# Scales of the gate and value weights from a partition's sum of magnitudes on ScalarE, in place of raw maxima on VectorE, with new issue times for that stage

## The chip, the core and the metric

The program runs on one core of a Trainium2 chip. The engines of the core work side by side, each through its own instructions in a fixed order: TensorE (PE, with its weight loads shown as PEld), VectorE (DVE), ScalarE (ACT), GpSimd (POOL) and SyncE (SP), which issues the DMAs here. Time is the device time of one execution in microseconds; less is better. A profiled execution also leaves a trace; its span is the time from the first to the last instruction.

## The reference

Attention whose scores are masked by hash buckets, then a gated feed-forward block, then a second feed-forward block. In the lines that matter:

```python
scores = np.where(mask, scale * np.matmul(q, k.transpose(0, 1, 3, 2)), -1e9)
attn = np.exp(scores - scores.max(-1, keepdims=True)); attn /= attn.sum(-1, keepdims=True) + 1e-9
x = np.matmul(attn, v)                        # 2 batches x 8 heads, 768 x 64 -> 1536 x 512
gate = 1 / (1 + np.exp(-(x @ w_gate)))        # 512 x 1536
x = (gate * (x @ w_val)) @ w_out              # the gate/value stage, then the w_out stage
h = x @ w_in                                  # second block, 512 x 2048
g = np.where(h >= 1, h, np.where(h <= -1, 0, (h + 1) ** 2 / 4))
out = g @ w_out2
```

Inputs are drawn normally; the gate weights are 188.518 times as large as the shapes would suggest.

## The kernel before

**Precision.** A product in full precision is made from 16-bit halves: each operand is split into a high and a low float16 part, and three matmuls (high by high, high by low, low by high, lines 421 to 423) are summed in PSUM. So that the weights keep within float16's range, each tile of weights is multiplied by a power of two. That power comes from the tile's own magnitudes, worked out on the chip.

**The gate/value stage.** The stage has twelve weight tiles, in the order g0, v0, g1, v1, ... g5, v5 (g a gate tile, v a value tile). Each tile is used for both batches, which gives 24 groups of work, numbered k = 0 to 23: k = 0 and 1 are g0, k = 2 and 3 are v0, k = 4 and 5 are g1, and so on. A group is an object `Quad`. It makes four blocks of output by a scheme with seven products instead of eight, `P(0)` to `P(6)`, each six matmuls of 128x384. The products accumulate in PSUM banks called qa, qe, qb, qc and qd. Since one product serves several blocks, ScalarE copies a bank into the next (`seed`: qa to qb, qb to qc, qb to qd, line 386) and keeps qe in SBUF (`keep5`, line 372). TensorE's P(2) waits for the first copy, P(4) for the second and P(6) for the third. VectorE adds (line 402), ScalarE applies the tanh of the gate (line 389), VectorE multiplies (line 392).

**What a weight tile goes through.** The input arrives as two raw tiles `wr` (`a_load`, three DMAs on SP, lines 309 to 312), in 64-bit words whose high and low words are converted into one float32 tile `wt` of 128x1024 on the chip: magnitudes on ScalarE (`a_abs`, line 164, two), range on GpSimd (`w_range`, line 167), a shift on VectorE (line 170), low words (line 173, two) and sign (line 176, two). The scale takes its own way: `a_max` takes the largest raw high word of each partition from each raw tile (two reductions, line 265), joins the two (line 267), and `row_out` sends the 128 numbers by DMA into one row (line 256). `row_in` then reduces that row on VectorE (line 239), masks the exponent (line 240), does three small GpSimd steps (lines 242, 243, 246) and sends the scale by DMA to all partitions (line 261). With `wt` and the scale, `a_sum` makes sums of quarter tiles (`ws`, line 334), `a_hi` writes the high parts on ScalarE (line 342: `a` of 128x768 and two `s` of 128x512), `a_lo` the low parts on VectorE (line 350). The raw tiles have two buffers per kind: gate tiles share one pair, value tiles from v1 on another, so a load waits until the last reader of the tile before it is done.

**What sets the order.** Every step is put on a list with a program time, in units of one product; the list is sorted and the instructions are issued in that order. `on` and `at` put a step on the list. The tables hold the times: `F0`, `AT` and `AM` for the attention's pairs of heads, `QP` for the steps of a group (seeds, sums, acts), `WP` for the steps of a weight tile. A time decides nothing but the place in the engines' queues; on each queue the order is strict, and semaphores hold a waiting instruction and all behind it. The end of attention is written by hand as well: there the first gate groups (k = 0 and 1) are threaded between the last attention steps, the evacuations of the attention output (line 718, VectorE: `xr` from `O`) free the one PSUM bank `O` for the next output, and the casts of line 153 and the subtractions of line 131 split the attention output into high and low parts. For g0 the tile is made long before, within attention. Steps `g_load` and `g_max` (lines 206 and 209) read weights of later stages for their own scales, spread over this stage.

## Time and profile before

| | |
|---|---|
| median of 3 runs | 761.7 us (761.12 to 762.7) |
| profiled execution: time / span | 759.33 us / 757.5 us |
| granted TensorE clock, mean | 0.994 |
| PE busy | 728.7 us, 96% of the span, 4883 matmuls |
| DVE busy | 648.1 us, 86% |
| ACT busy | 521.1 us, 69% |
| POOL busy | 227.5 us, 30% |

TensorE is idle for 28.8 us of the span in all (757.5 less 728.7). The time outside the span is 1.83 us. Attention lasts to about 237 us with the first two gate groups within its end, the gate/value stage to about 404 us, the w_out stage to about 460 us, and the second block to the end.

### The profile page before, as it was taken

What the parts mean: (1) busy time and instruction counts of PE and PEld (TensorE: products, weight loads), DVE (VectorE), ACT (ScalarE), POOL (GpSimd) and SP (SyncE); (2) the same over time, 40 slices, a digit from 0 to 9 for tenths busy, and PEclk for the clock granted to TensorE, in tenths of its full rate; (3) what the DMA queues carried; (4) which work ended last, traced back from release to release, by engine and by line L of the source; (5) the groups of instructions that cost most, each with busy time, mean ns of one, the idle gap of its engine ahead of it and who ended that gap; (6) DMA issues with size and microseconds to landing.
All of it is one profiled execution on the core that took longest, in us unless ns stands there. A gap on an engine that the chain in (4) does not pass through costs nothing.

```text
span 757.5 us, 13220 instructions
## 1 busy us (share of the span) xinstructions
PE 728.7 (96%) x4883; PEld 461.5 (61%) x4883; DVE 648.1 (86%) x1141; ACT 521.1 (69%) x985; POOL 227.5 (30%) x311
## 2 busy tenths in 40 slices
PE   7899999999998999998999999998999999999997
PEld 4778878888885555555555556664555555555553
DVE  6899999889888989998889999999999996766643
ACT  6789889988885674673764445546776677767753
POOL 6435267774685653463430001103000000000000
PEclk9999999999999999999999999999999999999999
DMA  8564554454302155556565913533333200100002
GB/s 253 157 184 113 137 146 121 106 128 100 100 1 56 57 180 197 178 170 209 180 230 199 406 56 112 168 112 113 110 112 94 73 1 29 57 0 1 1 1 83
DMA packets 53200, 89.59 MB, mean 118 GB/s; under 512 B 9872, under 2 KB 33040, under 8 KB 53136
## 3 DMA queue, kind: packets, MB, share of 16 engines
q1 hardware_dynamic: 52400, 88.07, 37.8%
q8 instruction: 38, 0.62, 0.3%
q10 hardware_dynamic: 736, 0.69, 0.3%
q14 instruction: 26, 0.21, 0.1%
HBM read 68.65 MB, written 3.15 MB: 95 GB/s over the span
## 4 chain that ended last, share of the span: by engine, by line
PE 35%; DVE 22%; DMA 4%; ACT 3%; issue 2%; POOL 1%; SPq 1%; ACTq 0%; DVEq 0%; POOLq 0%
DVE h L131 2%; PE p L423 2%; PE p L422 2%; PE p L421 2%; DMA gi<-in_moe_w_in_dram 2%; PE qa L1357 2%; DVE gmx L209 2%; PE qa L1356 2%; PE qa L1355 2%; PE qe L1356 2%; PE qe L1355 2%; PE qe L1357 2%; PE o L1356 2%; PE o L1357 2%; PE o L1355 2%; DVE h L392 2%
## 5 line engine op out<-in xcount | busy, mean ns | idle before, releaser
L643 DVE SCALAR_TENSOR_TENSOR PT<-pt,PT 128x512 f16<-128x512 f32 x144 | 95.2, 681 | 8.5 <-ACT PT L640 7.0
L605 DVE TENSOR_REDUCE st<-sc 128x1 f32<-128x768 f32 x96 | 90.7, 948 | 6.5 <-PE sc L597 5.5
L609 ACT ACTIVATE P<-sc,st 128x768 f32<-128x768 f32 x96 | 87.1, 908 | 8.7 <-DVE st L605 7.9
L640 ACT ACTIVATE PT<-pt 128x512 f16<-128x512 f32 x144 | 82.2, 599 | 11.4 <-PE pt L631 9.7
L631 PE MATMUL pt<-ident,P 128*128 128x128 f32 x576 | 80.9, 279 | 0.8 <-DVE PT L643 0.5
L631 PEld LDWEIGHTS pt<-ident,P 128*128 128x128 f32 x576 | 65.4, 142 | 13.7 <-issue 8.8
L709 PE MATMUL O<-PT,vh 128*64 128x256 f16 x576 | 54.4, 277 | 2.1 <-DVE xr L718 2.1
L421 PE MATMUL p<-y,i 128*128 128x384 f16 x128 | 41.7, 326 | 0.0
L422 PE MATMUL p<-y,i 128*128 128x384 f16 x128 | 41.7, 326 | 0.0
L423 PE MATMUL p<-y,i 128*128 128x384 f16 x128 | 41.7, 326 | 0.0
L709 PEld LDWEIGHTS <-vh 128*64 128x64 f16 x576 | 31.0, 109 | 15.1 <-issue 14.6
L1357 PEld LDWEIGHTS <-g 128*128 128x128 f16 x192 | 18.9, 98 | 25.1 <-DVE g L131 2.3
L709 PE MATMUL O<-PT,vl 128*64 128x256 f16 x288 | 33.8, 273 | 0.0
L242 POOL TENSOR_SCALAR row<-row 1x1 uint32<-1x1 uint32 x15 | 5.5, 369 | 91.0 <-DVE row L240 90.9
L597 PE MATMUL sc<-N,N 128*128 128x384 f32 x96 | 29.3, 386 | 3.1 <-ACT N L533 1.9
L1334 ACT ACTIVATE t<-p,usc 128x384 f32<-128x384 f32 x32 | 21.3, 665 | 15.9 <-PE p L423 15.8
L1355 PEld LDWEIGHTS <-g 128*128 128x128 f16 x192 | 18.9, 98 | 21.3 <-ACT g L1344 1.3
L421 PE MATMUL y<-h,w_o 128*128 128x384 f16 x96 | 31.3, 326 | 0.4 <-DVE h L392 0.4
L1356 PEld LDWEIGHTS <-g 128*128 128x128 f16 x192 | 18.9, 98 | 20.5 <-issue 0.8
L423 PE MATMUL y<-h,w_o 128*128 128x384 f16 x96 | 31.3, 326 | 0.0
L422 PE MATMUL y<-h,w_o 128*128 128x384 f16 x96 | 31.3, 326 | 0.0
L597 PE MATMUL sc<-H,H 128*128 128x384 f32 x96 | 28.9, 382 | 2.3 <-ACT P L609 2.2
(355 smaller groups left out, 2292.8 us busy)
## 6 DMA issues: line engine op xcount, KB each, us to landing
wr_o<-in_moe_w_out_dram SPq DMA_DIRECT2D x28, 512.0 KB, 4.6
gi<-in_moe_w_in_dram SPq DMA_DIRECT2D x21, 384.0 KB, 4.8
gz<-in_moe_w_out_dram SPq DMA_DIRECT2D x21, 384.0 KB, 7.5
go<-in_moe_w_out_dram SPq DMA_DIRECT2D x16, 384.0 KB, 4.6
H<-U SPq DMA_DIRECT2D x28, 192.0 KB, 3.3
wr_i<-in_moe_w_in_dram SPq DMA_DIRECT2D x8, 512.0 KB, 3.8
wr_i<-in_moe_w_in_dram SPq DMA_DIRECT2D x16, 256.0 KB, 3.0
n<-in_qt_dram SPq DMA_DIRECT2D x8, 384.0 KB, 4.3
```

Source lines behind the costliest of these rows:

```text
L421: nc.tensor.matmul(ps, lhsT=wh, rhs=rh, start=first, stop=False, **kw)
L422: nc.tensor.matmul(ps, lhsT=wh, rhs=rl, start=False, stop=False, **kw)
L423: nc.tensor.matmul(ps, lhsT=wl, rhs=rh, start=False, stop=last, **kw)
L605: nc.vector.tensor_reduce(out=self.st[:, 0, self.c:self.c + 1], in_=self.sc[:, :, 0:HN], op=ALU.max, axis=AX.XY, negate=True)
L609: nc.scalar.activation(out=self.P, in_=self.sc[:, :, 0:HN], func=AF.Exp, bias=self.st[:, 0, self.c:self.c + 1], scale=1.0, accum_out=self. ...
L631: nc.tensor.transpose(self.ps[m][:, j, :], un[2 * self.n + e].P[:, a, c:c + 128], ident)
L640: nc.scalar.activation(out=self.part(0, m), in_=self.ps[m], func=AF.Copy, scale=PSCALE)
L643: nc.vector.scalar_tensor_tensor(out=self.part(1, m), in0=self.ps[m], scalar=PSCALE, in1=self.part(0, m), op0=ALU.mult, op1=ALU.subtract)
L709: nc.tensor.matmul(O_ps[r, 0:GN], lhsT=vv[m][:, e, i * D:(i + 1) * D], rhs=PT[:, l, e * NI + i, :], start=(s == 0), stop=(s == len(steps) ...
L1355: nc.tensor.matmul(OA[b][i], lhsT=gh[:, ts], rhs=wh, start=(fc == ORD2[0]), stop=False)
L1356: nc.tensor.matmul(OA[b][i], lhsT=gh[:, ts], rhs=wl, start=False, stop=False)
L1357: nc.tensor.matmul(OA[b][i], lhsT=gl[:, ts], rhs=wh, start=False, stop=(fc == ORD2[-1]))
```

## The change

For the ten tiles g1 to v5 the two reductions and the joining step on VectorE go. In their place ScalarE runs one pass over the finished float32 tile `wt`, with the absolute value as its function and an accumulator that sums each partition's magnitudes (`a_norm`). Its element output goes into the tile's first raw buffer, which nothing reads any more. The row of 128 sums is then treated as a row of float32 numbers: `row_in` is called without the 64-bit form, so `exponents` has two GpSimd steps in place of three, and with 0 in place of 14 as the headroom (`lead`). The tiles g0 and v0 keep `a_max`. The times of the stage are new: loads of gate tiles stand 3.6 and of value tiles 6.2 units earlier, conversions earlier, the row and the scale later, seeds, sums and acts moved; so are the steps around the end of attention, and some in `F0`, `AT`, `AM`. The spacing of the `g_load` and `g_max` steps of the weights "i" goes from 3.1293 to 2.7251.

```diff
+    def a_norm(t):
+        x, raw = wsc[:, a_num(t)], WO[t]["raw"][0]
+        nc.scalar.activation(out=raw.bitcast(F32), in_=WO[t]["wt"], func=AF.Abs, accum_out=x[:, 0:1])
+        row_out(t, x[:, 0:1])
+
     def a_row(t):
-        row_in(t, wsc[:, a_num(t), 2:4], 14.0, True)
+        first = a_num(t) < 2
+        row_in(t, wsc[:, a_num(t), 2:4], 14.0 if first else 0.0, first)
...
             for i in range(2):
-                at(11.9 + 0.65 * i, 0, last, a_abs, "v0", i)
+                at(11.6588 + 0.65 * i, 0, last, a_abs, "v0", i)
                 at(10.8628 + 0.7012 * i, 0, last, a_max, "v0", i)
-            for i, t in enumerate((13.0012, 13.3012, 13.6012, 13.4, 13.85, 14.0)):
+            for i, t in enumerate((12.9754, 13.2754, 14.0754, 13.8742, 16.8242, 17.0000)):
                 at(t, 0, last, a_conv, "v0", i)
...
     for m in range(4):
-        on(7.9432, a_sum, V, "v0", m, True)
-    on(5.7405, a_row, "v0")
-    on(9.4664, a_scale, "v0")
+        on(6.3628, a_sum, V, "v0", m, True)
+    on(4.1807, a_row, "v0")
+    on(5.5893, a_scale, "v0")
...
     QP = {
-        "g": {"seed": (0.4974, 2.358, 4.976), "p5": 3.5377, "sum": (3.99, 5.128, 7.1683, 8.1683), "act": (5.4565, 7.5607, 8.0579, 7.094)},
-        "v": {"seed": (0.3623, 2.8959, 5.4602), "p5": 2.4313, "sum": (3.0782, 5.7535, 7.5389, 6.9122), "act": (3.7144, 5.3665, 5.5617, 6.5916)},
+        "g": {"seed": (0.2651, 2.2467, 4.976), "p5": 3.4485, "sum": (3.99, 5.5247, 6.8017, 8.1683), "act": (5.6194, 7.2386, 8.2511, 6.6591)},
+        "v": {"seed": (0.0402, 2.5738, 5.5827), "p5": 3.5552, "sum": (4.5242, 7.1995, 7.9195, 7.2928), "act": (4.095, 5.5833, 4.7321, 4.9298)},
     }
...
-        "g": {"load": -12.353, "abs": (-7.6756, -6.6904), "conv": (-6.1199, -4.6189, -4.5466, -4.3686, -4.145, -0.7947), "max": (-7.5452, -5.621), "row": -4.3568, "scale": 7.9278, "sum": (-0.0892, 0.724, 1.0886, 3.3024), "hi": (4.4351, 4.7082, 6.3431), "lo": (4.8041, 8.8601, 7.6451)},
-        "v": {"load": -14.3264, "abs": (-6.6935, -4.8952), "conv": (-4.4301, -3.9593, -2.346, 0.2172, -1.0263, 2.9987), "max": (-6.0592, -5.6294), "row": -1.4716, "scale": 9.9234, "sum": (3.1886, 3.5668, 5.287, 4.3833), "hi": (10.4857, 10.7314, 12.6551), "lo": (11.9836, 12.2806, 15.7582)},
+        "g": {"load": -15.9707, "abs": (-12.8785, -9.6904), "conv": (-9.1199, -7.7042, -7.6319, -6.7554, -7.0417, -3.7947), "max": -3.6384, "row": -1.4984, "scale": 6.1142, "sum": (-3.3668, -1.9704, -1.9242, 0.4534), "hi": (4.8637, 5.8088, 7.4437), "lo": (5.4761, 10.7242, 9.9904)},
+        "v": {"load": -20.5181, "abs": (-7.9256, -7.3055), "conv": (-6.2317, -5.7609, -4.8939, -2.091, -3.7825, -1.0482), "max": 0.5348, "row": 5.4491, "scale": 9.753, "sum": (0.4177, 0.7959, 2.287, 1.3833), "hi": (8.9311, 10.3557, 12.6551), "lo": (11.9836, 12.2806, 13.8746)},
     }
...
-        for m, d in enumerate(T["max"]):
-            on(base + d, a_max, n, m)
+        on(base + T["max"], a_norm, n)
```

Lines after the new function stand six higher in the changed program: 386 becomes 392, 342 becomes 348, 718 becomes 724.

**VectorE at the end of attention.** The rows begin where the last weight steps of v0 meet the last attention steps; `xr_2` from `O_3_1` is the evacuation for which the attention's next output waits. Before:

```order
L615 RECIPROCAL st_3_0_4_3353<-st_3_0_4_3353 128x4
L170 TENSOR_SCALAR wt_v_3519<-wt_v_3519 128x1024
L239 TENSOR_REDUCE row_78<-row_78 1x1
L173 SCALAR_TENSOR_TENSOR wt_v_3519<-wr_v_3168,wt_v_3519 128x512
L173 SCALAR_TENSOR_TENSOR wt_v_3519<-wr_v_3167,wt_v_3519 128x512
L643 SCALAR_TENSOR_TENSOR PT_3_2_3434<-pt_2_3548,PT_3_2_3434 128x4x128
L176 SCALAR_TENSOR_TENSOR wt_v_3519<-wr_v_3167,wt_v_3519 128x512
L176 SCALAR_TENSOR_TENSOR wt_v_3519<-wr_v_3168,wt_v_3519 128x512
L240 TENSOR_SCALAR row_78<-row_78 1x1
L334 TENSOR_TENSOR ws_v_3731<-wt_v_3519 128x256
L334 TENSOR_TENSOR ws_v_3731<-ws_v_3731,wt_v_3519 128x256
L718 SCALAR_TENSOR_TENSOR xr_2_3163<-O_3_1_3505,rs_3_1_3_3490 128x256
```

And now:

```order
L170 TENSOR_SCALAR wt_v_3505<-wt_v_3505 128x1024
L649 SCALAR_TENSOR_TENSOR PT_3_2_3434<-pt_2_3548,PT_3_2_3434 128x4x128
L173 SCALAR_TENSOR_TENSOR wt_v_3505<-wr_v_3168,wt_v_3505 128x512
L173 SCALAR_TENSOR_TENSOR wt_v_3505<-wr_v_3167,wt_v_3505 128x512
L239 TENSOR_REDUCE row_78<-row_78 1x1
L176 SCALAR_TENSOR_TENSOR wt_v_3505<-wr_v_3167,wt_v_3505 128x512
L240 TENSOR_SCALAR row_78<-row_78 1x1
L724 SCALAR_TENSOR_TENSOR xr_2_3163<-O_3_1_3507,rs_3_1_3_3490 128x256
```

The evacuation now stands in front of the second sign step and of all four sums of v0.

**ScalarE where the second gate group (k = 1) begins.** The last rows before the copy of qa into qb, on which TensorE's P(2) waits. Before:

```order
L153 CAST pT_1_3599<-xT_1_3314 128x384
L389 ACTIVATE h_0_3557<-h_0_3557,wsc 128x384
L386 ACTIVATE qb_3728<-qa 128x384
L389 ACTIVATE h_0_3557<-h_0_3557,wsc 128x384
L389 ACTIVATE h_0_3557<-qd_3675,wsc 128x384
L153 CAST pB_1_3715<-xr_2_3163 128x384
L153 CAST pT_1_3718<-xt_3313 128x384
```

And now:

```order
L153 CAST pT_1_3596<-xT_1_3314 128x384
L395 ACTIVATE h_0_3557<-h_0_3557,wsc 128x384 x2
L395 ACTIVATE h_0_3557<-qd_3675,wsc 128x384
L153 CAST pT_1_3716<-xt_3313 128x384
L164 ACTIVATE wt_g_3724<-wr_g_3619 128x512
L392 ACTIVATE qb_3738<-qa 128x384
```

One tanh has become two in front of the copy, and a third tanh, a cast and a magnitude step have come to stand ahead of it.

**ScalarE in the second group of a gate tile (k = 5, tile g1).** From the first copy of this group to that of the next. Before:

```order
L386 ACTIVATE qb_4050<-qa 128x384
L389 ACTIVATE h_1_3964<-h_1_3964,wsc 128x384 x2
L386 ACTIVATE qc_4073<-qb_4050 128x384
L342 ACTIVATE a_v_4092<-wt_v_3887,wsc 128x768
L372 ACTIVATE p_g_1_4094<-qe 128x384
L342 ACTIVATE s_v_4096<-ws_v_4006,wsc 128x512
L386 ACTIVATE qd_4104<-qb_4050 128x384
L389 ACTIVATE h_1_4040<-qa,wsc 128x384
L342 ACTIVATE s_v_4096<-ws_v_4006,wsc 128x512
L389 ACTIVATE h_1_4040<-qd_4104,wsc 128x384
L386 ACTIVATE qb_4142<-qa 128x384
```

And now:

```order
L392 ACTIVATE qb_4049<-qa 128x384
L395 ACTIVATE h_1_3954<-h_1_3954,wsc 128x384
L348 ACTIVATE a_v_4066<-wt_v_3874,wsc 128x768
L392 ACTIVATE qc_4074<-qb_4049 128x384
L348 ACTIVATE s_v_4084<-ws_v_3967,wsc 128x512
L272 ACTIVATE wr_g_3933,wsc<-wt_g_3981 128x1024
L378 ACTIVATE p_g_1_4088<-qe 128x384
L392 ACTIVATE qd_4098<-qb_4049 128x384
L395 ACTIVATE h_1_4040<-qa,wsc 128x384
L348 ACTIVATE s_v_4084<-ws_v_3967,wsc 128x512
L395 ACTIVATE h_1_4040<-qd_4098,wsc 128x384
L392 ACTIVATE qb_4136<-qa 128x384
```

The new pass for g2 (line 272) and the high parts of v1 now stand between the copies into qc and qd.

**SP between two weight loads.** Rows of the DMA queue up to the load of gate tile g3; `row_76` there is the scale row of v2. Before:

```order
L256 DMA row_76<-wsc 1x128x1
L206 DMA go_4235<-in_moe_w_out_dram 128x384
L206 DMA go_4272<-in_moe_w_out_dram 128x384
L261 DMA wsc<-row_76 128x1x2
L309 DMA wr_g_4313<-in_moe_w_gate_dram 128x4x128
L311 DMA wr_g_4314<-in_moe_w_gate_dram 128x2x128
L312 DMA wr_g_4314<-in_moe_w_gate_dram 128x2x128
```

And now, where `row_78` is the scale row of g2 and `row_76` again that of v2:

```order
L261 DMA wsc<-row_78 128x1x2
L206 DMA go_4148<-in_moe_w_out_dram 128x384
L206 DMA go_4182<-in_moe_w_out_dram 128x384
L206 DMA go_4224<-in_moe_w_out_dram 128x384
L315 DMA wr_g_4260<-in_moe_w_gate_dram 128x4x128
L317 DMA wr_g_4261<-in_moe_w_gate_dram 128x2x128
L318 DMA wr_g_4261<-in_moe_w_gate_dram 128x2x128
L206 DMA go_4266<-in_moe_w_out_dram 128x384
L256 DMA row_76<-wsc 1x128x1
L206 DMA go_4308<-in_moe_w_out_dram 128x384
L206 DMA go_4344<-in_moe_w_out_dram 128x384
L261 DMA wsc<-row_76 128x1x2
```

The load of g3 stood behind the scale of v2 and now stands in front of it.

## Rows read from the trace of the kernel before

**Rows 1.** The page: busy time of each engine, share of the span, instructions.

```profile
PE 728.7 (96%) x4883; PEld 461.5 (61%) x4883; DVE 648.1 (86%) x1141; ACT 521.1 (69%) x985; POOL 227.5 (30%) x311
```

**Rows 2.** Waits of PE, whole span: who waited for whom, us, times, longest.

```profile
PE qb L421 <- ACT qb L386: 3.6, 3, 2.2
...
PE qb L421 <- ACT qc L386: 1.2, 3, 0.8
...
PE qb L423 <- DVE s_g L350: 0.5, 1, 0.5
```

**Rows 3.** Windows: stretch, length, then busy us (count) of PE, PEld, DVE, ACT, POOL.

```profile
270.00:290.00 20.00, 20.00 (x125) 12.02 (x124) 17.88 (x33) 15.69 (x30) 11.31 (x15) 1.00 0.57 186
```

**Rows 4.** Groups of DVE by line, 239 to 404 us: count, busy us, mean ns.

```profile
L265 DVE TENSOR_REDUCE wsc<-wr_g 128x1 f32<-128x512 f32 x10 | 6.7, 680 | 1.8 <-DMA wr_g<-in_moe_w_gate_dram 1.6
```

**Rows 5.** Timeline of ACT, weight tile v0's high parts: start, length.

```profile
247.45 0.93 ACT L342 ACTIVATE a_v<-wt_v,wsc 128x768 f16<-128x768 f32 x1
248.28 0.71 ACT L342 ACTIVATE s_v<-ws_v,wsc 128x512 f16<-128x512 f32 x1
```

**Rows 6.** Timeline of ACT in attention: an accumulator's read, the next instruction.

```profile
63.85 0.21 ACT L609 ACTIVATION_READ_ACCUMULATOR P<-sc,st 128x1 f32 x1
64.07 0.90 ACT L609 ACTIVATE P<-sc,st 128x768 f32<-128x768 f32 x1
```

**Rows 7.** Timeline of ACT at a late load; in brackets the idle time before.

```profile
358.45 0.68 ACT L164 ACTIVATE wt_g<-wr_g 128x512 f32<-128x512 f32 x1 [2.41 <-DMA wr_g<-in_moe_w_gate_dram]
359.02 0.58 ACT L389 ACTIVATE h<-qd,wsc 128x384 f32<-128x384 f32 x1
359.96 0.69 ACT L164 ACTIVATE wt_g<-wr_g 128x512 f32<-128x512 f32 x1 [0.36 <-DMA wr_g<-in_moe_w_gate_dram]
360.53 0.51 ACT L386 ACTIVATE qb<-qa 128x384 f32<-128x384 f32 x1
```

**Rows 8.** Timeline of SP's queue ahead of that load.

```profile
352.46 0.48 SPq L261 DMA_DIRECT2D wsc<-row  x1
...
353.67 0.38 SPq L309 DMA_DIRECT2D wr_g<-in_moe_w_gate_dram  x1
```

**Rows 9.** Timeline of PE at the end of attention and in k = 1.

```profile
237.49 0.30 PE L709 MATMUL O<-PT,vh 128*64 128x256 f16 x2 [2.11 <-DVE xr L718]
...
244.42 0.32 PE L421 MATMUL qb<-pT,s_g 128*128 128x384 f16 x1
...
249.42 0.34 PE L421 MATMUL qd<-pT,a_g 128*128 128x384 f16 x1 [0.66 <-ACT qd L386]
```

**Rows 10.** Timeline of DVE ahead of that evacuation, and two later sums.

```profile
233.41 2.78 DVE L176 SCALAR_TENSOR_TENSOR wt_v<-wr_v,wt_v 128x512 uint32<-128x512 uint32 x2
...
236.22 0.42 DVE L334 TENSOR_TENSOR ws_v<-wt_v 128x256 f32<-128x256 f32 x1
...
237.02 0.42 DVE L718 SCALAR_TENSOR_TENSOR xr<-O,rs 128x256 f32<-128x256 f32 x1
...
243.73 0.55 DVE L402 TENSOR_TENSOR h<-qc,p_g 128x384 f32<-128x384 f32 x1
```

**Rows 11.** Timeline of ACT at the start of k = 1.

```profile
243.90 0.47 ACT L386 ACTIVATE qb<-qa 128x384 f32<-128x384 f32 x1
```

**Rows 12.** DMA issues, 240 to 400 us: count, KB each, median us to landing.

```profile
row<-wsc SPq DMA_DIRECT2D x10, 0.5 KB, 1.9
wsc<-row SPq DMA_DIRECT2D x10, 1.0 KB, 2.3
```

**Rows 13.** Timeline of ACT at the start of the w_out stage.

```profile
402.51 0.72 ACT L1115 ACTIVATE w_o<-wf_o,hsc 128x512 f16<-128x512 f32 x1 [3.08 <-DVE wf_o L176]
```

**Rows 14.** Timeline of PE: attention's second pair, and the second block.

```profile
52.74 0.62 PE L597 MATMUL sc<-N,N 128*128 128x384 f32 x2 [1.03 <-ACT P L609]
...
517.26 0.61 PE L1357 MATMUL qa<-w,g 128*128 128x512 f16 x1 [1.83 <-DVE g L131]
```

**Rows 15.** Window around the second of these; last three: granted clock, DMA share, GB/s.

```profile
516.00:520.00 4.00, 2.74 (x7) 1.04 (x8) 3.97 (x10) 2.94 (x6) 0.09 (x1) 0.59 0.43 131
```

More of the change, by code (lines that the diff above doesn't have):

```diff
@@ L792, in lsh_attention_glu_act @@
             F0 = {
-                "max": (0.835, 4.3363, 4.8113, 6.0),
+                "max": (0.6194, 4.3363, 4.8113, 6.0),
                 "first": (1.1116, 1.92, 2.6321, 2.6521),
@@ L800, in lsh_attention_glu_act @@
                 "MAX": (-0.86, 0.21, 0.88, 1.91, 2.7, 4.3082, 4.6882, 5.3482, 7.3656, 9.7482, 9.8482, 8.9617),
-                "EXP": (0.22, 0.6565, 1.1565, 2.5865, 2.8165, 4.4, 4.86, 7.05, 8.14, 10.5074, 11.21, 9.27),
[1 row of a table removed]
+                "EXP": (0.22, 0.6565, 1.1565, 2.5865, 2.8165, 4.4, 4.86, 6.3485, 8.14, 10.5074, 11.21, 9.27),
[1 row of a table added]
                 "HI": (1.61, 2.61, 4.28, 4.75, 2.76, 6.16, 4.82, 7.1271, 8.1731, 9.03, 9.58, 10.42, 9.66, 11.6, 11.38, 12.5, 12.62, 12.77),
[1 row of a table removed]
[1 row of a table added]
                 "ST": (4.8549, 8.95, 13.1659),
@@ L825, in lsh_attention_glu_act @@
             AM = {
-                "QK": (-1.6212, -0.312, 0.1234, 1.0922, 0.2911, 4.4841, 2.6311, 3.1388, 4.9681, 7.5662, 8.3203, 9.8239),
+                "QK": (-1.6212, -0.312, 0.1234, 1.0809, 0.2911, 4.4841, 2.6311, 3.1388, 4.9681, 7.5662, 8.3203, 9.8239),
                 "MAX": (-0.8384, -0.282, 0.274, 2.0221, 1.7029, 4.7833, 2.832, 3.457, 5.7284, 8.6318, 8.8402, 9.9223),
-                "EXP": (-0.0169, 0.1389, 0.7054, 2.7327, 1.7202, 5.1256, 3.1579, 4.9368, 7.4948, 9.0696, 9.801, 10.9635),
+                "EXP": (-0.0169, 0.1389, 0.7054, 2.7327, 1.7202, 5.1256, 3.1579, 4.6699, 7.4948, 9.0696, 9.801, 10.9635),
                 "T": (0.6726, 2.7818, 2.4903, 2.8259, 5.6069, 4.8189, 4.5978, 6.1506, 6.3992, 8.0591, 8.0212, 8.3198, 10.1114, 11.2138, 10.6646, 10.8685, 12.1144, 12.284),
[1 row of a table removed]
[1 row of a table added]
                 "LO": (2.054, 4.2198, 3.2826, 5.2606, 7.9391, 5.7821, 5.4721, 7.5402, 7.967, 9.0285, 8.7977, 9.5983, 10.7969, 12.174, 11.1739, 12.0774, 12.8392, 13.9848),
@@ L846, in lsh_attention_glu_act @@
                 "V4": (8.2939,),
-                "RB": (7.5895, 9.9185, 12.8309),
-                "VR": (7.1203,),
-                "VT": (10.3243,),
-                "STP": (6.1912, 6.7323, 11.461),
+                "RB": (7.5895, 8.88, 11.7924),
+                "VR": (6.0818,),
+                "VT": (9.2858,),
+                "STP": (5.1527, 6.7323, 11.461),
             }
@@ L1406, in lsh_attention_glu_act @@
         on(6.0 + 0.1 * i, x_op, 1, op, C0, P, True)
-    on(8.106, x_op, 1, "hB22", C1, nc.scalar, True)
-    on(8.3, x_op, 1, "lB22", C1, V, True)
-    on(8.2, x_op, 1, "hT4", C1, nc.scalar, True)
-    on(8.4715, x_op, 1, "lT4", C1, V, True)
+    on(8.4549, x_op, 1, "hB22", C1, nc.scalar, True)
+    on(8.598, x_op, 1, "lB22", C1, V, True)
+    on(5.9953, x_op, 1, "hT4", C1, nc.scalar, True)
+    on(6.0085, x_op, 1, "lT4", C1, V, True)
     for m in range(4):
-        on(7.9432, a_sum, V, "v0", m, True)
@@ L1413, in lsh_attention_glu_act @@
-    on(5.7405, a_row, "v0")
-    on(9.4664, a_scale, "v0")
+        on(6.3628, a_sum, V, "v0", m, True)
+    on(4.1807, a_row, "v0")
+    on(5.5893, a_scale, "v0")
     on(11.1344, a_hi, "v0", "a", 0, True)
-    on(11.4975, a_lo, "v0", "a", 0, True)
+    on(12.195, a_lo, "v0", "a", 0, True)
     for m in range(2):
-        on(11.1514 + 3.1136 * m, a_hi, "v0", "s", m, True)
-        on(11.5944 + 3.0944 * m, a_lo, "v0", "s", m, True)
+        on(10.7952 + 3.0212 * m, a_hi, "v0", "s", m, True)
+        on(11.2174 + 2.7382 * m, a_lo, "v0", "s", m, True)
@@ L1423, in lsh_attention_glu_act @@
     }
     WP = {
-        "g1": {"abs": (-1.9247, -3.3264), "conv": (-1.6834, -1.2227, 2.2696, 1.9568, 2.5568, 2.5305), "max": (-5.2173, -4.5384), "row": 0.0204, "scale": 8.7461, "sum": (3.1461, 4.5686, 3.894, 5.4285), "hi": (11.5982, 11.5142, 12.628), "lo": (12.1178, 11.9436, 16.9718)},
-        "g": {"load": -12.353, "abs": (-7.6756, -6.6904), "conv": (-6.1199, -4.6189, -4.5466, -4.3686, -4.145, -0.7947), "max": (-7.5452, -5.621), "row": -4.3568, "scale": 7.9278, "sum": (-0.0892, 0.724, 1.0886, 3.3024), "hi": (4.4351, 4.7082, 6.3431), "lo": (4.8041, 8.8601, 7.6451)},
@@ L1427, in lsh_attention_glu_act @@
-        "v": {"load": -14.3264, "abs": (-6.6935, -4.8952), "conv": (-4.4301, -3.9593, -2.346, 0.2172, -1.0263, 2.9987), "max": (-6.0592, -5.6294), "row": -1.4716, "scale": 9.9234, "sum": (3.1886, 3.5668, 5.287, 4.3833), "hi": (10.4857, 10.7314, 12.6551), "lo": (11.9836, 12.2806, 15.7582)},
+        "g1": {"abs": (-6.2649, -7.6772), "conv": (-6.0342, -5.5735, -2.0812, -1.2283, -0.3001, -0.4695), "max": 0.9384, "row": 3.5384, "scale": 9.6277, "sum": (0.1461, 1.5513, 0.8767, 3.6183), "hi": (12.1986, 12.1146, 13.2626), "lo": (13.5502, 12.3696, 17.4819)},
@@ L1458, in lsh_attention_glu_act @@
     end = 14 * NT
-    for w, (t0, dt) in {"o": (29.7834, 3.4864), "i": (86.3431, 3.1293), "z": (154.0638, 2.0141)}.items():
+    for w, (t0, dt) in {"o": (29.7834, 3.4864), "i": (86.3431, 2.7251), "z": (154.0638, 2.0141)}.items():
         for k in range(g_num(w)):
```

4 lines of the change are left out of this document (2 added, 2 removed), and 12 rows, old and new, of tables (AM, AT).

## The prediction, made before the changed kernel was run

> **What bounds the kernel now.** I read the page first: TensorE is busy 96% of the span, VectorE 86%, ScalarE 69% [rows 1]. So time can be won only where TensorE stands still (28.8 us in all), and lost wherever a new wait reaches it. Next came the list of what TensorE waits for, and the timeline around each wait. In the gate/value stage the reader is to see that VectorE is almost never the one waited for: the longest such wait is one of 0.5 us, while the copies of the banks on ScalarE (qa to qb, qb to qc) cost 3.6 and 1.2 us [rows 2]. The timeline of ScalarE tells why. At 358.45 and 359.96 the magnitude steps of a gate tile have waited 2.41 and 0.36 us for a load, and the copy into qb stands behind them [rows 7]; TensorE lost 2.19 us there, the longest wait of the first row [rows 2]. SP's queue shows why the load was late: it was issued at 353.67, right behind the scale DMA of the value tile at 352.46 [rows 8]. Of the waits on qb and qc (4.8 us), I found 3.6 us (2.19, and two shorter) behind such late loads. At the end of attention two more waits stand out: 2.11 us for an evacuation on VectorE and 0.66 us for a copy into qd [rows 9].
>
> **What is removed.** Ten tiles lose two reductions of 0.68 us each [rows 4], 13.6 us of VectorE (the small joining steps aside). Worth on the path: hardly more than the 0.5 us wait of row s_g [rows 2], since elsewhere VectorE's idle time hides it. I take 0.7 us, for that wait and two shorter ones on VectorE; bounds 0 and 0.9.
>
> **What is added.** One pass of 128x1024 on ScalarE for each of the ten tiles, with an accumulator. No such pass is in the trace. The 128x768 pass takes 0.93 us and the next instruction starts 0.83 us after it; a 128x512 pass takes 0.71 [rows 5]. So 256 elements more cost 0.22 us, and 1024 take about 0.83 + 0.22 = 1.05 us of the queue. Attention's EXP, which has an accumulator too, is followed by a read that holds the queue from 63.85 to 64.07, 0.22 us [rows 6]. Bounds are 1.05 and 1.27; I take 1.2, nearer to the row with a read. Ten are 12 us of ScalarE, in a stage where a stretch without any wait of TensorE has ScalarE busy 15.7 of 20 us [rows 3].
>
> Does it fit? In that stretch 125 matmuls fill 20 us, 0.16 us each, so a group of 42 lasts 6.7 to 6.8 us. In the second group of a gate tile ScalarE now has three copies, four tanh, one 128x768 pass, two 128x512 passes, one copy of qe and the new pass between one copy into qb and the next. In queue time (each about 0.08 to 0.1 less than its length) that is 3 x 0.41 + 4 x 0.49 + 0.83 + 2 x 0.62 + 0.4 + 1.2 = 6.9 us [rows 5, 7, 11], just over the group. The new pass and the high parts stand between the copies into qc and qd, so the copy into qd ends 0.1 to 0.6 us after P(6) could start. A tanh can slip into the next group, so it does not pile up. Five such groups, at about 0.16: a loss of 0.8 us; bounds 0 and 2.5. A value tile's pass stands in the first group of a gate tile, between the copies into qb and qc, where no high part stands: by the same count 0.1 to 0.8 us are free there. I set it at nothing; without that cover it would be 0.1 to 0.5 us for each of five.
>
> The Trainium skill, "ScalarE: Activation LUTs", section "What ACT_TABLE_LOAD costs", gives an ACTIVATE with immediates as 186 ns and 0.833 ns an element, with about 93 ns of overlap between neighbours. The rows' slope (0.22 us for 256) agrees; by the page alone the pass would be an estimated 0.95 us of the queue, the group 6.6 us, and the loss of 0.8 nothing, so that the time would be 756.7.
>
> **The scale comes later.** The sum needs the finished tile, so row, exponent and scale follow the second sign step. The two DMAs land after 1.9 and 2.3 us [rows 12]; with the reduce and the small steps between them about 5 to 6 us pass from the new pass to the scale. VectorE stands at the reduce of the row (line 239) for up to 2 us; behind it wait sums and products of banks that come due later, and the removed 1.36 us a tile cover most of that. SP stands at line 256 and line 261 as it did before. GpSimd has one small step less a tile. All this I set at nothing; if the scale of a value tile is late, its first high part is, and the sum loses up to 0.5 us a tile.
>
> **Loads.** A gate tile's load no longer stands behind the value tile's scale, but behind the scale of the gate tile before, with three other loads between; that is most of a group earlier. Its buffer is free once the new pass and the sign steps of the tile before are done, which is ahead of that scale. So the late loads vanish, though ScalarE's magnitude steps have moved earlier too. Gain 3.5 us of 3.6; bounds 2.5 and 3.6.
>
> **The end of attention.** The evacuation at 237.02 stood behind two sign steps (2.78 us for both) and two sums of 0.42 [rows 10]. One sign step and both sums now stand behind it: 1.39 + 0.84 = 2.2 us earlier, and the 2.11 us wait goes [rows 9]. But TensorE then runs into the copy into qb for k = 1. Before, that copy began at 243.90 right after one tanh, and P(2) at 244.42 [rows 9, 11]. Now it stands behind a second tanh, which needs the sum that ended at 244.28 (243.73 + 0.55) [rows 10], a third tanh, a cast and a magnitude step. Taking 2.11 off that sum gives 242.17; then 0.5 + 0.5 + 0.4 + 0.6 for these, and 0.47 for the copy, end near 244.65. P(2) starts near 244.7, 0.27 us later than before, so the whole 2.11 is spent in a new wait of some 2.4 us. The wait of 0.66 for qd goes, since P(6)'s copy is no longer behind two weight passes. In k = 2 and k = 3 more is late: the low part of v0 comes behind line 170 of g1, which waits for GpSimd, and TensorE loses 0 to 0.5 us; the new pass of g1 waits for its last sign step, with the copy into qc behind it, 0 to 0.8 us. Taking the middles: 0.66 - 0.27 - 0.25 - 0.45 = -0.3 us. Bounds: -1.5 and +2.1, the latter if the copy is not held.
>
> **The rest.** The conversion of the w_out weights moves up; ScalarE waited 3.08 us for it with the copy into qb behind [rows 13], which cost TensorE 0.84 us. Gain 0.8; bounds 0 and 0.84. In attention's second pair the reductions of g0 stand later in VectorE's queue and no longer delay a row maximum; a wait of 1.03 us [rows 14] shrinks by some 0.4 (bounds 0 and 1). The other moved steps of attention keep their places but for a few neighbours: nothing, within 0.5 either way.
>
> **Sum.** 3.5 + 0.7 - 0.8 - 0.3 + 0.8 + 0.4 = 4.3 us. Against the profiled execution (span 757.5 and 1.83 around it, 759.33 us) that gives 755.0. The median of the runs is 2.4 us above that execution, so I take the same off the median: 761.7 - 4.3, rounded to **757.5**.
>
> **The rivals.** (a) *The queue of ScalarE takes it back: no measurable change.* For: ScalarE's second gate group is full by my count, and the pass waits for a sign step in front of two copies. Against: the 3.6 us of late loads are long single waits, and the new ones would be short. With 0.5 us in each of five groups (2.5) and the end of attention at -1.5, the gain is 3.5 + 0.4 + 0.8 - 4.0 = 0.7: 761.0.
>
> (b) *Slower: the second gate group is bound by ScalarE.* Place: the copies into qc and qd behind the new pass. If the pass waits for its sign step in each gate tile and for the scale in each value tile, 0.8 us for each of ten, it loses 8 against at most 5: 764.5. It decides from about 0.6 us for each of ten. Against: a gate tile's conversion begins 5 units earlier than before, so its sign step should be done.
>
> (c) *The clock.* In the second block a wait of 1.83 us [rows 14] has the granted clock at a mean of 0.59 over 4 us [rows 15], which costs 0.41 x 4 = 1.6 us of matmuls, while the waits of 2.11 and 2.19 us fell at full clock. The new 2.4 us wait at k = 1 could bring the low level, 1.2 GHz in place of 2.4: 757.5 + 1.6 = 759.1. The Trainium skill, "TensorE: Matmul & The Clock Gate", section "HAM oscillation — how this bites in real kernels", says that idle gaps throttle the clock again; the trace agrees at 516 us and not at the other two.
>
> (d) *The end of attention gains its 2.1.* If the copy into qb comes in time: 757.5 - 2.4 = 755.1, and 753.5 if the second gate groups lose nothing besides.
>
> **How the numbers follow.** The forecast with its own spread (756 to 759) has 0.45, (c) 0.10, (d) 0.18, (a) 0.16, (b) 0.11. Faster by over 0.2% (1.5 us, about what a measurement of this kernel can tell from no change) are the forecast, (c) and (d), and a little of (a): 0.75. Within 0.2% is most of (a): 0.14; slower is (b): 0.11. The range goes from 753.5, the end of (d), to 762, just past (a); it leaves out (b) and a few in 100 below.
>
> **What would show it.** Right: no wait of ScalarE for a gate load; no wait of about 2 us for the evacuation, and one of about 2.4 us at P(2) of k = 1; the new pass at 1.1 us with a read of 0.2; waits of TensorE for the copy into qd below 0.6 us in the second gate groups. Wrong: many waits of TensorE on qc or qd behind line 272, high parts of value tiles that wait for the scale DMA, ScalarE still idle for loads, or a clock below full after k = 1.

## The result, and the profile after

The changed kernel takes 753.4 us (752.45 to 754.25, 4 runs), the kernel before 762.2 us (761.12 to 764.0) in the same comparison: ratio 0.9879, 95% interval 0.9857 to 0.9902, so 7.5 to 10.9 us faster. In a second comparison of the same two kernels the ratio was 0.9902 (0.9874 to 0.9930). The forecast was 757.5 in a range from 753.5 to 762, so 753.4 lies just outside it. The direction was right; the gain was about twice the forecast.

The two profiled executions stand 6.73 us apart (759.33 and 752.60). The busy times differ little but for VectorE, ScalarE and GpSimd; the line answers to [rows 1]:

```profile
PE 727.3 (97%) x4883; PEld 461.7 (61%) x4883; DVE 639.5 (85%) x1111; ACT 530.9 (71%) x1005; POOL 220.5 (29%) x301
```

VectorE's busy time falls by 8.6 us only, though reductions of 13.6 us are gone: other steps of the stage took longer, such as the twelve low parts `s_v` (line 356), with a mean of 888 ns in place of 735. Why they did is open.

What TensorE waits for, whole span (columns as in [rows 2]):

```profile
PE qb L427 <- ACT qb L392: 2.3, 1, 2.3
...
PE qd L427 <- ACT qd L392: 1.2, 4, 0.4
...
PE qb L427 <- ACT qc L392: 0.6, 3, 0.3
```

The 3.6 us behind late loads (2.19, 0.85 and 0.58) are gone, and so is the 0.5 us for s_g. The first line is a new wait at k = 1, forecast at 2.4 us. Of the four waits in the second line, three are for the copy into qd in second gate groups: 0.17, 0.32 and 0.32 us, 0.81 in all, where 0.8 was forecast. The fourth, 0.38 us, is in the last value group.

ScalarE at the start of k = 1, then TensorE's P(2) (timeline; answers to [rows 9, 11]):

```profile
240.21 0.61 ACT L395 ACTIVATE h<-h,wsc 128x384 f32<-128x384 f32 x1 [0.32 <-DVE h L408]
240.73 0.56 ACT L395 ACTIVATE h<-qd,wsc 128x384 f32<-128x384 f32 x1
241.19 0.50 ACT L153 CAST pT<-xt 128x384 f16<-128x384 f32 x1
241.59 0.66 ACT L164 ACTIVATE wt_g<-wr_g 128x512 f32<-128x512 f32 x1
242.15 0.48 ACT L392 ACTIVATE qb<-qa 128x384 f32<-128x384 f32 x1
...
242.69 0.32 PE L427 MATMUL qb<-pT,s_g 128*128 128x384 f16 x1 [2.33 <-ACT qb L392]
```

The copy ends at 242.63 behind the tanh, cast and magnitude step that the change put in front of it. The granted clock then falls; the window after it answers to [rows 15]:

```profile
243.00:248.00 5.00, 5.00 (x23) 2.56 (x21) 5.00 (x8) 3.44 (x8) 1.79 (x2) 0.66 0.36 124
```

A mean of 0.66 over 5 us, between the two levels of 1.2 and 2.4 GHz, is up to 1.7 us of matmuls lost. So in this trace the fall of the clock of rival (c) came on top of the wait that the forecast had; its time, 759.1, did not.

The second group of tile g1 (timeline of ScalarE):

```profile
273.78 0.47 ACT L392 ACTIVATE qc<-qb 128x384 f32<-128x384 f32 x1
274.19 0.70 ACT L348 ACTIVATE s_v<-ws_v,wsc 128x512 f16<-128x512 f32 x1
274.80 1.04 ACT L272 ACTIVATE wr_g<-wt_g 128x1024 f32<-128x1024 f32 x1
275.75 0.19 ACT L272 ACTIVATION_READ_ACCUMULATOR wr_g<-wt_g 128x1 f32 x1
275.84 0.47 ACT L378 ACTIVATE p_g<-qe 128x384 f32<-128x384 f32 x1
276.21 0.47 ACT L392 ACTIVATE qd<-qb 128x384 f32<-128x384 f32 x1
```

The new pass holds the queue from 274.80 to 275.84, 1.04 us with its read, which is the lower of the bounds that the prediction gave (1.05), where it took 1.2.

Where the 6.73 us are, by places that both traces have: attention from the small matmul of line 655 (now 661) near 18 us to the third-last evacuation, then the first product of v0 (250.48 and 249.24), then the first product of the w_out stage into its bank `y` (411.31 and 405.70), 2 to 2.5 us after that stage's first products of all:

| part | before | after | gain | forecast |
|---|---|---|---|---|
| start | 18.65 | 18.41 | 0.24 | 0 |
| attention | 206.78 | 205.08 | 1.70 | 0.4 |
| end of attention, k = 0 and 1 | 25.05 | 25.75 | -0.70 | 0.4 |
| k = 2 to the w_out stage | 160.83 | 156.46 | 4.37 | 3.5 |
| the rest | 346.2 | 345.1 | 1.1 | 0 |

(The forecast's terms are put to the rows: 0.66 - 0.27 for the end of attention; 3.5 + 0.7 - 0.8 + 0.8 and the 0.7 lost in k = 2 and 3 for the row below.) The last row is the clock: the 1.83 us wait of [rows 14] is there after the change too, but the clock stays at its upper level behind it this time. Over all the traces of this document, the last part takes 346.2 to 346.6 us in the five with that fall and 344.0 to 345.1 in the twelve without.

Attention's 1.70 us have a second place besides the one forecast. VectorE near 103 us, before and after:

```profile
103.09 0.96 DVE L605 TENSOR_REDUCE st<-sc 128x1 f32<-128x768 f32 x1 [0.40 <-PE sc L597]
103.97 1.75 DVE L176 SCALAR_TENSOR_TENSOR wt_g<-wr_g,wt_g 128x512 uint32<-128x512 uint32 x1
105.64 0.68 DVE L643 SCALAR_TENSOR_TENSOR PT<-pt,PT 128x512 f16<-128x512 f32 x1
```

```profile
100.73 0.68 DVE L649 SCALAR_TENSOR_TENSOR PT<-pt,PT 128x512 f16<-128x512 f32 x1
101.33 1.20 DVE L176 SCALAR_TENSOR_TENSOR wt_g<-wr_g,wt_g 128x512 uint32<-128x512 uint32 x1
102.45 0.94 DVE L611 TENSOR_REDUCE st<-sc 128x1 f32<-128x768 f32 x1
```

A sign step of g0 stood behind a row maximum and held up what followed; now it stands in the gap ahead of that maximum, where VectorE waited 0.40 us, and takes 1.20 in place of 1.75.

### The profile page after: what moved, and what is told of

It is laid out like the page before. It is cut to its first block, busy times and chain, and to the rows that moved or that the text cites. A ratio compares the mean times of both kernels' runs of the same rounds, so it can differ in the third digit from the quotient of the medians.

```text
span 750.8 us, 13224 instructions
## 1 busy us (share of the span) xinstructions
PE 727.3 (97%) x4883; PEld 461.7 (61%) x4883; DVE 639.5 (85%) x1111; ACT 530.9 (71%) x1005; POOL 220.5 (29%) x301
## 4 chain that ended last, share of the span: by engine, by line
PE 33%; DVE 13%; DMA 2%; ACT 1%; issue 1%; SPq 0%; POOL 0%; ACTq 0%
PE p L427 2%; PE p L429 2%; PE p L428 2%; DVE h L131 2%; PE qa L1363 2%; PE o L1363 2%; PE qa L1362 2%; PE o L1362 2%; PE o L1361 2%; PE qa L1361 2%; PE qe L1363 2%; PE qe L1362 2%; PE qe L1361 2%; DMA gz<-in_moe_w_out_dram 1%; DVE w_o L1124 1%; DVE vmx L1215 1%
## 5 line engine op out<-in xcount | busy, mean ns | idle before, releaser
L1121 ACT ACTIVATE w<-wf_z,gsc 128x512 f16<-128x512 f32 x16 | 11.5, 721 | 25.0 <-DVE wf_z L176 25.0
```

## The experiments

Times are medians; a ratio is always to the kernel before, in the same comparison. "The stage" is the time from the first product of v0 to the first one into `y` in the run's own trace, as in the table.

### The kernel before, again

> The kernel before, unchanged, traced a second time. Spread theory: the executions differ by how long the late loads hold ScalarE and by whether the TensorE clock falls, so a second trace shows other sums than 3.6 us behind late loads (up to 6 us), and the median stays 2 to 3 us above the 759.3 us of the first trace. Rival, a fixed offset between a traced and an untraced execution: the same 3.6 us of stalls again, and every trace near 759.

760.76 us (758.6 to 765.82), ratio 1.0001 (0.9974 to 1.0028). Its trace has a span of 762.9 us, 5.4 longer than the first, and other late loads. The waits of TensorE from 245 to 416 us, and one of them with its neighbour on TensorE:

```profile
PE qb L421 <- ACT qb L386: 6.1, 4, 2.7
...
303.98 0.48 PE L421 MATMUL qb<-pT,s_g 128*128 128x384 f16 x1 [2.73 <-ACT qb L386]
304.25 0.53 PE L422 MATMUL qb<-pT,s_g 128*128 128x384 f16 x1
```

```profile
303.00:309.00 6.00, 5.02 (x21) 2.60 (x21) 5.51 (x11) 4.54 (x9) 2.64 (x4) 0.72 0.26 71
364.00:370.00 6.00, 5.22 (x22) 2.72 (x22) 4.53 (x10) 4.48 (x10) 2.11 (x3) 0.72 0.35 108
```

6.1 us where the first trace had 3.6 in that line (0.84 us of each is the start of the w_out stage), and behind two of the waits the clock falls to a mean of 0.72 over 6 us, 1.7 us each. The stage takes 165.62 us against 160.83. So the two traces differ as the spread theory had it, by late loads and by the clock behind them, and the first trace was one of the shorter executions. The median came 1.4 us above it, not 2 to 3.

### The changed kernel, again

> The changed kernel, unchanged, traced a second time. Theory that the change takes out the waits which vary from run to run (late loads in front of the copies of banks): its runs spread over less than 4 us where those of before spread over 9.5 (757.24 to 766.73), the median is 752 to 755, and no wait of ScalarE for a gate load is over 0.5 us in the second trace. Rival, a lucky first set: a spread like that of before and a median of 755 to 758.

753.69 us (752.1 to 754.43), ratio 0.9902 (0.9874 to 0.9930); stage 158.80 us. No wait of ScalarE for a gate or value load appears in its trace. The 6 runs spread over 2.3 us, the 23 of before in the same comparison over 7.5 (757.03 to 764.52).

### Attention's moved steps alone

The new tables F0 and AM and the new list of g0's steps go into the kernel before, nothing else; of the edit only the list is shown:

```diff
-                q, t = ((1, 1.3756), (1, 2.5756), (1, 5.1058), (2, 2.7058), ...
+                q, t = ((1, 2.1099), (1, 3.3099), (1, 5.8401), (2, 2.7058), ...
```

> The kernel before with only the new tables F0 and AM and the new steps of g0 within attention. Theory that these moves pay by themselves: 1.5 to 2.1 us faster than before, all of it by 150 us of the span (about 0.7 at 46 to 56 us, about 1.0 at 103 to 108 us). Rival, that the prediction's 0.4 us was right and the rest came by chance from run to run: 0 to 0.5 us.

759.97 us, ratio 0.998 (0.996 to 1.0001): 1.5 us faster, 0 to 3, with an interval that just takes in no change. In the trace attention takes 204.27 us, against 205.66 in the second trace of before, which has the clock at the same level at 25 us as this one. So 1.4 us, nearer to the new theory than to 0.4.

### The changed kernel with attention's old steps

The reverse edit, in the changed kernel.

> The changed kernel with the old tables F0 and AM and the old steps of g0 in attention. If the new ones pay by themselves: 1.3 to 2.1 us slower than the changed kernel, 755 to 756, all of it before 150 us of the span. Rival, chance from run to run: within 0.5 us of it.

754.5 us, ratio 0.9907 (0.9882 to 0.9932): 0.8 to 1.1 us over the two medians of the changed kernel, with intervals that overlap. Attention takes 205.39 us, 1.46 more than in the second trace of the changed kernel (203.93). The place is settled by the traces; the size by clock time only roughly.

### Load times alone

```diff
-        "g": {"load": -12.353,
+        "g": {"load": -15.9707,
-        "v": {"load": -14.3264,
+        "v": {"load": -20.5181,
```

> The kernel before with only the two load times of the changed kernel, so that a gate load stands in front of the value tile's scale DMA. Stall theory: the waits on qb behind late loads go (3.6 us in the first trace), 2.5 to 5 us faster than before. Rival, the loads are held by the DMA engines and not by their place in the queue: the same waits of ScalarE for a gate load, 0 to 1 us.

760.35 us, ratio 0.9989 (0.9968 to 1.0009): no gain that can be told. ScalarE no longer waits for gate loads, but TensorE has new waits for the low part a_v (3.26, 1.04 and 0.54 us), and behind the longest the clock falls (a mean of 0.69 from 337.5 to 343). SP's queue and VectorE show why:

```profile
328.99 0.38 SPq L309 DMA_DIRECT2D wr_v<-in_moe_w_val_dram  x1
...
330.53 0.50 SPq L256 DMA_DIRECT2D row<-wsc  x1
...
335.37 0.27 DVE L239 TENSOR_REDUCE row<-row 1x1 f32<-1x128 f32 x1 [2.74 <-DMA row<-wsc]
```

The row of 0.5 KB, issued behind a whole weight load, lands 4.8 us later, where the median was 1.9 [rows 12]; VectorE stands for it with the low parts behind. The place of the loads alone only moves the wait.

### The new times with the raw maxima, late and early

Both are the changed kernel with `a_max` in place of `a_norm`, and with the row in its 64-bit form again; first the maxima stand at the place of the pass, then at their old times. The central lines of the second edit:

```diff
-        on(base + T["max"], a_norm, n)
+        for m, d in enumerate(T["max"]):
+            on(base + d, a_max, n, m)
```

> The changed kernel with the raw maxima on VectorE again, at the place of the new pass, so that the new times stand without the new source of the scale. Stall theory (the gain is earlier loads and moved steps, VectorE is hardly waited for): within 1.5 us of the changed kernel, 7 to 10 us faster than before; it may even be faster, since ScalarE loses 12 us of work. Rival, VectorE's relief is what pays: 3 us or more of the gain go, with waits of TensorE on VectorE of over 2 us in the stage.

> The changed kernel with the raw maxima on VectorE at their old times, all other new times kept, so that the scale is ready early and VectorE carries its 13.6 us again while ScalarE is free of the new pass. If VectorE's relief is what makes the new times work: the waits of the run with late maxima stay for the most part (copies into qc and qd held behind sums of VectorE, 4 us or more), 758 to 762. If only the late place of the maxima held up that run: within 1.5 us of the changed kernel, 752 to 755.

762.0 us, ratio 1.0012 (0.9995 to 1.0030), and 761.41 us, ratio 1.0006 (0.9987 to 1.0025). The whole gain is gone in both, though both keep the attention steps; the stage takes 165.88 and 166.24 us, where the old times with the maxima had 160.83 and 165.62. In the first run ScalarE waits for no gate load any more, and still TensorE loses 6.8 us in four waits for copies into qc. My stall theory, by which the new times earn the gain, falls. One wait of the second run, on VectorE and ScalarE:

```profile
302.38 0.69 DVE L173 SCALAR_TENSOR_TENSOR wt_g<-wr_g,wt_g 128x512 uint32<-128x512 uint32 x1
302.99 0.68 DVE L265 TENSOR_REDUCE wsc<-wr_g 128x1 f32<-128x512 f32 x1
303.59 0.55 DVE L407 TENSOR_TENSOR h<-qc,p_g 128x384 f32<-128x384 f32 x1
```

```profile
304.17 0.61 ACT L394 ACTIVATE h<-h,wsc 128x384 f32<-128x384 f32 x1 [1.40 <-DVE h L407]
305.50 0.93 ACT L347 ACTIVATE a_v<-wt_v,wsc 128x768 f16<-128x768 f32 x1 [0.72 <-DMA wsc<-row]
306.34 0.47 ACT L391 ACTIVATE qc<-qb 128x384 f32<-128x384 f32 x1
```

A tanh waits 1.40 us for a sum that stands behind a maximum, the high part waits 0.72 us for its scale (0.15 to 0.53 us in the first trace of the changed kernel), and the copy into qc stands behind both: TensorE loses 1.93 us, and the view puts it down to ScalarE.

### The kernel before without its maxima

```diff
     def a_max(t, h):
+        if a_num(t) > 1:
+            if h == 1:
+                row_out(t, wsc[:, 0, 0:1])
+            return
```

> The kernel before with the maxima of the ten tiles g1 to v5 left out: their rows are sent from the column of g0, so the scales of these tiles are g0's. Old times, old loads. Relief theory (VectorE's 13.6 us hold up sums, conversions and the scale row, and through them ScalarE and the next load): the stage from the first product of v0 to the first of w_out falls from about 162 us (three traces: 160.8, 165.6, 159.7) to 158 or less, 3 us or more faster than before. The prediction's reading (VectorE hardly waited for): late loads stay, 0 to 1 us faster.

755.37 us, ratio 0.9934 (0.9906 to 0.9962): 2.9 to 7.2 us faster; stage 157.84 us. Old times, old loads, no pass on ScalarE, and the gain of the stage is there. A late load is there too, and TensorE waits behind it:

```profile
354.53 0.67 ACT L164 ACTIVATE wt_g<-wr_g 128x512 f32<-128x512 f32 x1 [1.73 <-DMA wr_g<-in_moe_w_gate_dram]
...
357.64 0.32 PE L425 MATMUL qb<-pT,s_g 128*128 128x384 f16 x1 [1.95 <-ACT qb L390]
```

So this gain is not that the late loads vanish. At this place the wait was 2.19 us before. Three other waits stand in both traces alike (0.50, some 0.85 and 0.38 us); what else TensorE waited in the stage comes to 2.2 us in the first trace of before (0.58 for qb, 1.16 for qc, 0.44 for VectorE) and to 0.15 us here. But here SP's queue is free of a wait too, so two more runs part VectorE's queue from that wait.

### Maxima that nobody waits for, and copies in their place

In the first the maxima are computed and the row is sent from g0's column; in the second each tile has one copy of 128 numbers at the place of the last maxima step. Both have g0's scale in ten tiles.

```diff
-            row_out(t, x[:, 0:1])
+            row_out(t, x[:, 0:1] if a_num(t) < 2 else wsc[:, 0, 0:1])
```

```diff
+            if h == 1:
+                nc.vector.tensor_copy(out=x[:, 0:1], in_=wsc[:, 0, 0:1])
+                row_out(t, x[:, 0:1])
+            return
```

> The kernel before, in which VectorE still computes the maxima of the ten tiles, but their rows are sent from the column of g0, so that SP's queue and the scales do not wait for them. If what the removal pays is the wait of SP's queue for the maxima (46.1 us in nine waits in the first trace, with the next loads behind): as fast as the run without maxima, 755 to 757. If it is VectorE's 13.6 us themselves: like before, 760 to 762.

> The kernel before, in which each tile's three maxima steps are one copy of 128 numbers (g0's column) on VectorE at the place of the last of them, so that SP's queue still waits for VectorE, which has 13 us less to do. If VectorE's time is what pays: as fast as the run without maxima, 755 to 757. If it is the wait of SP's queue by its place in the order: nearer to before, 758 to 761.

761.79 us, ratio 0.9997 (0.9975 to 1.0018), and 755.38 us, ratio 0.9922 (0.9891 to 0.9953). So it is VectorE's queue that pays, and not SP's wait. What these runs do not part is the 13.6 us of work and the time for which VectorE's queue stood in front of the maxima until a raw gate tile had landed (1.6 us in the first trace [rows 4]): without the maxima both go.

How it reaches the load shows at the load of [rows 8]; VectorE before, then VectorE and SP with the copy:

```profile
346.25 0.55 DVE L209 TENSOR_REDUCE gmx<-gi 128x1 f32<-128x384 f32 x1 [2.06 <-DMA gi<-in_moe_w_in_dram]
346.72 1.27 DVE L265 TENSOR_REDUCE wsc<-wr_v 128x1 f32<-128x512 f32 x2
...
351.19 0.14 DVE L240 TENSOR_SCALAR row<-row 1x1 uint32<-1x1 uint32 x1
```

```profile
344.90 0.55 DVE L209 TENSOR_REDUCE gmx<-gi 128x1 f32<-128x384 f32 x1 [0.28 <-DMA gi<-in_moe_w_in_dram]
345.37 0.14 DVE L267 COPY wsc<-wsc 128x1 f32<-128x1 f32 x1
...
348.65 0.14 DVE L240 TENSOR_SCALAR row<-row 1x1 uint32<-1x1 uint32 x1
```

```profile
349.92 0.48 SPq L261 DMA_DIRECT2D wsc<-row  x1
...
351.13 0.38 SPq L314 DMA_DIRECT2D wr_g<-in_moe_w_gate_dram  x1
```

```profile
302.53 0.32 PE L426 MATMUL qb<-pT,s_g 128*128 128x384 f16 x1 [1.47 <-ACT qb L391]
...
358.60 0.32 PE L426 MATMUL qb<-pT,s_g 128*128 128x384 f16 x1 [0.98 <-ACT qb L391]
```

The load goes out 1.2 us behind the scale DMA in both (353.67 behind 352.46, and 351.13 behind 349.92), and the scale DMA waits, through three small GpSimd steps, for the mask of line 240, which stands in VectorE's queue. Against TensorE's own progress (the first product of that group at 349.96 before, at 348.68 with the copy) the load goes out 1.26 us earlier: the 1.27 us of the two maxima ahead of the mask. TensorE's wait behind this load, 2.19 us before, is 0.98 us with the copy (the last rows above).

VectorE was not busy all along there: it had waited 2.06 us for a transfer of `gi`. The maxima count because they stand on the path from that transfer to the mask. And this is one load. Another costs 1.47 us in the same trace, and in the run without any maxima the load of this place went out only 0.34 us earlier by the same measure. How the relief is shared out among all the waits of the stage is not shown.

### The pass twice, and left out

```diff
-        nc.scalar.activation(out=raw.bitcast(F32), in_=WO[t]["wt"], func=AF.Abs, accum_out=x[:, 0:1])
+        for i in (1, 0):
+            nc.scalar.activation(out=raw.bitcast(F32), in_=WO[t]["wt"], func=AF.Abs, accum_out=x[:, i:i + 1])
```

> The changed kernel with the new pass run twice for each of its ten tiles; the first result is thrown away. If ScalarE is full in the second group of a gate tile, as the prediction counted: 0.7 to 1.2 us in each of five such groups, 4 to 7 us slower than the changed kernel. If ScalarE has slack there: under 1.5 us slower.

> The changed kernel with the new pass left out: rows are sent from the column of g0, so ten tiles have g0's scale. It tells what the pass costs. Prediction's reckoning: about 0.8 us for the first pass in ten tiles, so 752.5 to 753. If each pass costs its whole length as the second one did (10.5 us for ten): 743 to 746. The waits for the copy into qd of 0.32 us go in either case.

Twice: 764.19 us, ratio 1.0046 (1.0025 to 1.0068), 10.5 us over the changed kernel for ten more passes of 1.05 us. The waits of its stage:

```profile
PE qb L428 <- ACT qc L393: 7.1, 10, 1.9
PE qd L428 <- ACT qd L393: 6.0, 4, 1.5
```

Left out: 753.8 us, ratio 0.9905 (0.9879 to 0.9930), no faster than with it (its rows go out early as well, in the 64-bit form). The waits for qd in second gate groups are gone there, but those for copies into qc come to 1.9 us, against 0.6 and 1.4 in the two traces with the pass. The first pass costs nothing that can be told, the second its whole length: the pass just fills what ScalarE had free between the copies. The prediction's count fits: with 1.04 in place of 1.2 it is 6.7 us of work in a group of 6.7 to 6.8. Its loss of 0.8 us is inside what these two runs can tell. The Trainium skill, "ScalarE: Activation LUTs", section "What ACT_TABLE_LOAD costs", would have the pass at an estimated 0.95 us of the queue; the trace agrees for the pass itself (its read begins 0.95 us after it), and the read adds 0.09.

### Three attempts on ScalarE's queue

The copy into qb of k = 1 first (a cast with its subtraction and the magnitude steps of g1 move behind it); the gate passes behind the copy into qd; both, with g1's magnitude steps and pass moved behind copies into qc. The central lines:

```diff
-            on(s0 + d, q_op, k, "seed", m)
+            on(s0 + (0.01 if k == 1 and m == 0 else d), q_op, k, "seed", m)
```

```diff
-  "g": ... "max": -3.6384,
+  "g": ... "max": -1.95,
```

> The changed kernel with the copy into qb of the second group ahead of the third tanh, the cast and the magnitude step on ScalarE. Queue theory: the wait of 2.33 us at P(2) of k = 1 falls below 0.8 us, the clock stays at its upper level there, and the kernel gains 1.5 to 3.5 us on the changed one (750 to 752). Rival, the sums of VectorE or the conversion of g1 behind hold the next copies instead: the wait moves to k = 2, 0 to 0.7 us gained.

> The changed kernel with the pass of a gate tile behind the copy into qd in place of in front of it. Queue theory: the waits of 0.3 us for qd in the second gate groups go (four of 0.17 to 0.32 in a trace) and the scale, some 0.6 us later, still comes in time: 0.5 to 1.5 us faster than the changed kernel. Rival, the scale of the gate tile is then late for its high part: a wait in the value groups, no gain.

> The changed kernel with the copy into qb of k = 1 first, the magnitude steps of g1 behind the copy into qc, the pass of g1 behind that of k = 2, and the gate passes behind the copy into qd. If the waits at k = 1 and k = 2 (2.3 us, or 3.0 us in four when only the first copy was moved) come from ScalarE's queue alone: 2 to 4 us faster than the changed kernel, 750 to 752. Rival, GpSimd's range step and VectorE behind it hold the low parts of v0: under 1 us faster.

754.15, 754.44 and 754.6 us; ratios 0.9905, 0.9898 and 0.9908, each with an interval that holds the changed kernel's 0.9902. In the first the wait falls from 2.33 to 0.29 us and the clock stays up, and what was won there goes on:

```profile
240.12 0.32 PE L427 MATMUL qb<-pT,s_g 128*128 128x384 f16 x1 [0.29 <-ACT qb L392]
...
243.47 0.34 PE L427 MATMUL qb<-pT,s_g 128*128 128x384 f16 x1 [1.23 <-ACT qc L392]
...
245.89 0.32 PE L428 MATMUL qc<-pB,s_g 128*128 128x384 f16 x1 [0.63 <-DVE pB L131]
```

So the first rival holds. In the second run the waits for qd in second gate groups are gone (there had been three, not four), but the high parts of four gate tiles wait 0.50 to 0.54 us for their scale, and nothing is won. In the third VectorE stands 1.94 us for GpSimd's range step of g1, with the low part of v0 behind it, for which TensorE waits 0.58 us. No version here can be told from the changed kernel.

## Why the prediction was wrong, by its steps

**What is removed: the step that failed.** It said that VectorE's 13.6 us were worth 0.7, "since elsewhere VectorE's idle time hides it", because TensorE is hardly ever seen to wait for VectorE. The runs without the maxima gained 5.0 and 5.9 us with everything else old, and the run whose maxima nobody waited for gained nothing. VectorE was late in a queue in which the mask of the scale row stands, and sums that ScalarE's tanh needs. What TensorE then waits for is the last link: a copy on ScalarE, behind a magnitude step, behind a load, behind SP's scale DMA, behind VectorE. I followed that chain back to SP's queue and stopped short of its end; SP's wait there was, through GpSimd, for VectorE's queue.

**Loads.** The gain of 3.5 us was put down to the new place of the loads. The mechanism came as forecast: wherever only the loads stand earlier, or all of the new times with the late maxima, ScalarE waits for no gate load (with the early maxima it does, up to 1.84 us). The price did not: the place alone gains 0.8 us (between a loss of 0.7 and a gain of 2.4), since TensorE then waits for low parts. The relief of VectorE alone, at old times, leaves waits behind late loads (1.95 us; 1.47 and 0.98 us) and still brings the stage to 157.84 and 158.24 us, against 160.83, 165.62 and 159.74 in three traces with the maxima, a mean of 162.1: so 4.0 us. The changed kernel, with both, has 156.46 and 158.80. So the two terms, 0.7 and 3.5, were wrong in their parts, and that their sum, 4.2, comes near the 4.0 us of the relief alone was luck.

**The rest: attention.** 0.4 us forecast, 1.7 in the traces, 1.5 by the run with the moved steps alone. "The other moved steps of attention keep their places but for a few neighbours: nothing" was the mistake: one neighbour, a sign step of g0, has some 1 us in the traces (the evacuation at 107.71 comes 8.03 us after the row maximum at 99.68, and 6.98 us after it now). No run moves this step alone.

**The median.** "I take the same off the median" assumed that an execution's distance to its profile is fixed. It is not: before spreads over 9.5 us (757.24 to 766.73 in 35 runs), and its two traces differ by late loads, which the changed kernel's traces do not have, and by the clock behind them. The first trace of before was 2.9 us below the 762.2 us of its comparison, that of after 0.8 us below 753.4. This 2.1 us and attention's 1.3 are most of the missing 4.5 us (8.8 measured, 4.3 forecast). The last part's 1.1 us, the clock at 510 us, differs from trace to trace, and the end of attention (1.1 less than forecast) and the stage (0.9 more) nearly cancel. The range did not follow from its terms either: (d) without the loss in the second gate groups is 757.5 - 2.4 - 0.8 = 754.3, not 753.5.

**What held.** The end of attention went as worked out: the wait of 2.11 us gone, one of 2.33 (2.4 forecast) at k = 1, the one of 0.66 gone. The clock fell there, which was rival (c): 1.34 us of the part's time (25.75 with the fall, 24.41 in a run without it). The w_out start and the waits for qd held in place and size. The later scale, set at nothing, cost little: ScalarE waits 1.8 us for it in five places, at most 0.53 us, though VectorE stands 11.3 us in all at the reduce of the row. Every sign that the prediction named for being right was there, and the time missed its range all the same: none of them bore on VectorE's share.
